# Retention attention and a multiplicative FFN in one kernel: the first dense step as plain products, with the first weights loaded by matrix and the second attention block's first unit moved up

## Chip, core and metric

One core of one Trainium2 chip runs the whole program. The metric is the device time of the program in microseconds (us): the median of several executions. Before the change it is 822.65 us (three runs, 821.73 to 824.22).

## What is computed

The inputs are float32 for the attention and float64 for the weights; the output is float32.

```python
# attention: B=8, H=8, S=576, D=64
scores = matmul(q, k.T) / sqrt(D)
ret    = scores * where(rel >= 0, gamma[h] ** rel, 0)      # causal decay per head
attn   = matmul(ret, v)
x      = attn.transpose(0, 2, 1, 3).reshape(B * S, H * D)  # 4608 x 512
# FFN: w1, w2 512 x 1024; w3 1024 x 1024; w_out 1024 x 512
out    = ((x @ w1) * (x @ w2)) @ w3 @ w_out
```

w3 and w_out are multiplied with each other first (`w3_mm`), so the last two products become one.

## The kernel before, in words

**Attention.** The batch is taken in pairs of two; a unit g is one pair and one chunk of the sequence (a short chunk of 64 rows, then four of 128). The units 0 to 4 are the first pair and are what this change reorders. Each unit goes through the same steps: `load` issues the DMAs of k, q and v (L145), `scale` multiplies q or v by the decay powers (L265 on GpSimd or VectorE, L263 in eight pieces on ScalarE), `front` transposes k and q on TensorE (L279) and copies them out of PSUM on ScalarE (L282), `score` multiplies them (L294) and applies the mask on VectorE (L297), `pv_state` and `pv` make the output (L336, L363) and a function that copies it to `xT` on ScalarE (L370), and `state` adds k and v into the running state (L317, copied at L321).

**Weights.** The float64 weights come in blocks of 128 x 512 numbers: `load_block` issues the DMAs on SyncE's queue into one of five `raw` buffers, and a block is turned into float32 in two halves. `begin_block` makes the exponent (three ScalarE activations L465 to L467, or, for one block, one VectorE instruction L461 and two activations) and the mantissa (VectorE L469, L472); `end_block` joins them (VectorE L483, L496). A generator `conversion` holds that order, and `convert(n)` and `convert_up_to(n)` advance it by so many steps wherever the program calls them. Blocks 0 to 15 are w1 and w2, 16 to 23 w_out, 24 to 39 w3. The first four blocks (key "A") hold 128 columns of w1 and the same 128 of w2 each; the other twelve (key "w12") hold 256 columns of one matrix.

**Dense steps.** `up(i, n, fp)` makes a quarter fp (256 columns of w1 and w2) for one group of 2 x 192 tokens (i, n) by a Strassen-Winograd scheme: seven block products of four matmuls each, 128 x 192, 28 in all (L596), with VectorE additions out of PSUM (L601), two ScalarE copies (L609, L624) and at the end the product of the w1 and the w2 result (L630). It needs the weight sums S1 to S4 of its quarter (`strassen_weights`, four VectorE instructions, L203) and the token sums of its group (`strassen_tokens`, L567). S3 is written over the block A21, and T3 over a block of the tokens. Between its products it advances the conversion (`conv`) and calls what lies in the list `aside`.

**Order.** The order of every engine's instructions is the order in which the program is written (a manual schedule); nothing reorders it later. It matters most in the first 160 us: units 0 to 4, twelve calls of `up` and the conversion of 26 blocks are interleaved by hand, and VectorE and ScalarE run their instructions in that order. Then come the eight `w3_mm` (64 matmuls of 128 x 512, L547), each of which needs one transposed pair of w3 blocks (L500). SyncE's queue carries the loads of k, q, v and of all blocks in program order, and a load whose buffer is still in use holds up those behind it. `keep_busy(n)` multiplies the identity with itself n times (L185), for no result. PSUM gives seven banks to all of this and one to the running state.

Of the kernel before, what the change touches and what calls it, by code (L numbers as in the profile page):

```python
# [8 lines left out]
F32 = mybir.dt.float32  # L9
# [33 lines left out]
def kernel(  # L43
# [338 lines left out]

    blocks = [(("A", r, f), None) for f in range(2) for r in range(2)]
    for fp in range(1, NQ):
        for j, w in enumerate((moe_w1, moe_w2)):
            for r in range(2):
                blocks.append((("w12", fp, j, r), w))
# [5 lines left out]
    def load_block():  # L395
        n = loaded[0]
        if n == len(blocks):
            return
        key, w = blocks[n]
        t = raw.tile([P, CV, 2], I32, tag="raw", name="raw", bufs=5)  # L400
        if key[0] in ("A", "w12"):
            if key[0] == "A":
                _, r, f = key
                t4 = t.rearrange("p (j c n) t -> p j c n t", j=2, c=2)
                parts = [(t4[:, j], w[:, f * P:(f + 1) * P]) for j, w in enumerate((moe_w1, moe_w2))]
            else:
                _, fp, _, r = key
                parts = [(t.rearrange("p (c n) t -> p c n t", c=2), w[:, fp * QC:(fp + 1) * QC])]
            for t2, src in parts:
                src = src[2 * r * P:2 * (r + 1) * P]  # L410
                if r == 0:
                    nc.sync.dma_start(t2, src.rearrange("(c p) n t -> p c n t", p=P))
                else:
                    for half in range(2):
                        nc.sync.dma_start(t2[heads[half]],
                                          src.rearrange("(c a d) n t -> a d c n t", a=2, d=D)[1 - half])
# [12 lines left out]
    def converted_to(n):  # L429
        key, _ = blocks[n]  # L430
        if key[0] == "A":
            return A(0, {(0, 0): "A11", (1, 0): "A12", (0, 1): "A21", (1, 1): "A22"}[key[1:]]).rearrange(
                "p j c n -> p (j c) n")
        if key[0] == "w12":
            _, fp, j, r = key
            return wA[fp // 2][:, r, j, :, fp % 2 * QC:fp % 2 * QC + QC]
        if key[0] == "wo":
            return live["wo"][:, key[1], :]
        _, ft, h = key
        if h == 0:  # L440
            live["w3"] = pools["wst"].tile([P, P // BL, DF // CV, CV // QP], F32, tag="w3", name="w3", bufs=1)
        return live["w3"][:, :, h, :]

    def begin_block():
        n = begun[0]
        t = live["raw", n]
        lo, hi = t[:, :, 0], t[:, :, 1]
        top = t.rearrange("p n t -> p (n t)").bitcast(BF16).rearrange("p (n u) -> p n u", u=4)[:, :, 3]
        e = raw.tile([P, CV], I32, tag="exp", name="e")
        m = raw.tile([P, CV], I32, tag="man", name="m")  # L450
        vec = nc.vector

        half = e.bitcast(BF16).rearrange("p (n u) -> p n u", u=2)[:, :, 1]
        func = mybir.ActivationFunctionType
        if n == 2 * NQ - 1:

            vec.tensor_scalar(out=e, in0=hi, scalar1=1, scalar2=21,  # L461
                              op0=ALU.logical_shift_left, op1=ALU.logical_shift_right)
# [12 lines left out]
        begun[0] += 1  # L475
        yield

    def end_block():
# [8 lines left out]
        while not (key[0] in ("A", "w12") or "wo" in live and (key[0] == "wo" or key[1] < multiplied[0] + 3)):  # L487
            yield "wait"
        out, m, e = converted_to(n), m.bitcast(F32), e.bitcast(F32)
        if key[0] == "A":  # L490
            m, e = (x.rearrange("p (c n) -> p c n", c=4) for x in (m, e))
# [12 lines left out]

        if n >= 4:
            load_block()
        if key[0] == "w12" and key[2:] == (1, 1):
            yield from strassen_weights(key[1])
        yield

    def conversion():

        yield from begin_block()
        while converted[0] < len(blocks):
            if begun[0] < len(blocks) and converted[0] not in (1, 2, 3, 6, 7):
# [15 lines left out]
    def convert(n):  # L533

        for _ in range(n):
            if go_on() is not None:
                return
# [94 lines left out]
            convert(conv)  # L632

    aside, owed, beside = [], [], []

# [175 lines left out]
    keep_busy(4)  # L813
    front(0, "q")
    convert(2)
    score(0)
    scale(0, "v")
    state(0)
    convert_up_to(1)
    pv(0)()  # L820
    load(2, "kqv")
    load_block()
    load_block()
    convert_up_to(2)
    load_block()
    front(1, "k")
    keep_busy(4)
    scale(1, "q", engine=nc.vector)
    front(1, "q")
# [9 lines left out]
    next(weight_sums)  # L839
    pv(1)()  # L840
    keep_busy(4)
    load(3, "v")
    load_block()
    convert_up_to(4)
    token_sums = strassen_tokens(0, 0, nc.vector)
    next(token_sums)
    next(weight_sums)
    list(token_sums)
    list(weight_sums)
    aside.extend([lambda: scale(2, "q", True), lambda: front(2, "k"), lambda: None, lambda: front(2, "q")])  # L850
    scale(2, "v")
    up(0, 0, 0, conv=[0, 0, 2, 2, 2], tail=False, first=True)
    convert(1)
    score(2)
    state(2)
    scale(3, "q", True)
    load(4, "kq")
    front(3, "k")
    convert(3)
    scale(3, "v", engine=nc.vector)  # L860
    copies = pv(2)
    front(3, "q")
    convert(4)
    copies()
# [8 lines left out]
    front(4)  # L873
    convert(1)
    pv(3)()
    list(strassen_tokens(0, 1, nc.vector))
# [517 lines left out]
```

## Time and profile before

| what | value |
|---|---|
| median of three runs | 822.65 us |
| the profiled execution | 821.6 us, span of its instructions 819.5 us |
| TensorE matmul busy | 805.1 us, 98% of the span |
| VectorE busy | 524.4 us, 64% |
| ScalarE busy | 245.3 us, 30% |
| GpSimd busy | 216.2 us, 26% |
| mean granted TensorE clock | 0.994 |
| read from HBM / written | 92.09 MB / 22.28 MB |

The span runs from the first to the last instruction of the profiled execution; the 2.1 us around it belong to start and end. All times below are positions in this span or durations of instructions in it. A busy TensorE need not be at its full clock: the granted clock stands in a column of its own. A wait is listed with what ended it.

### The profile page before, as it was taken

The numbers are of one execution on the slowest core, as the hardware profiler recorded it, in microseconds if no ns is written. First come the engines' busy times: TensorE is split into PE (matmuls) and PEld (weight loads), VectorE is DVE, ScalarE is ACT, GpSimd is POOL, SyncE is SP. The second block draws the span as 40 slices with busy tenths as digits, with TensorE's granted clock in tenths as the row PEclk, the third lists the DMA queues.
The fourth block names the chain that finished last, engine by engine and source line by source line (L and its number), as shares of the span: only waits on it lengthen the run. The fifth ranks groups of instructions, "written<-read, shape, count | busy, mean of one in ns | idle before, by whom it ended". The sixth has DMA issues, their size and how long they took to land.

```text
span 819.5 us, 14497 instructions
## 1 busy us (share of the span) xinstructions
PE 805.1 (98%) x5673; PEld 698.9 (85%) x5673; DVE 524.4 (64%) x789; ACT 245.3 (30%) x442; POOL 216.2 (26%) x147
## 2 busy tenths in 40 slices
PE   7989999999999999999999999999999999999998
PEld 7989999844788999888888888888888888888887
DVE  4899999994446485756545766555575566545633
ACT  4787556572110112113222111233211112232100
POOL 1200020000100503205657013167541213464300
PEclk7999999999999999999999999999999999999999
DMA  9995354468027966755963686458646611342011
GB/s 194 229 222 143 80 119 137 116 201 258 13 55 118 240 173 170 230 139 147 231 175 134 156 139 127 83 156 214 183 162 134 117 52 71 136 168 101 1 52 51
DMA packets 225155, 115.32 MB, mean 141 GB/s; under 512 B 195768, under 2 KB 209336, under 8 KB 225088
## 3 DMA queue, kind: packets, MB, share of 16 engines
q1 hardware_dynamic: 172704, 93.40, 44.2%
q10 hardware_dynamic: 52384, 21.01, 11.8%
q8 instruction: 44, 0.72, 0.4%
q14 instruction: 23, 0.19, 0.1%
HBM read 92.09 MB, written 22.28 MB: 140 GB/s over the span
## 4 chain that ended last, share of the span: by engine, by line
PE 86%; DVE 6%; DMA 3%; SPq 2%; issue 2%; ACT 1%; POOL 0%; ACTq 0%; DVEq 0%; POOLq 0%
PE up L1056 27%; PE po L743 24%; PE up L596 13%; PE ps L547 7%; PE upz L1056 4%; PE xps L363 3%; PE sc L294 3%; DMA ld_v<-in_v_dram 2%; PE st L317 2%; PE xps L336 2%; SPq L893 1%; PE tp L279 1%; DVE pm L297 1%; DVE e L483 1%; DVE m L472 1%
## 5 line engine op out<-in xcount | busy, mean ns | idle before, releaser
L1079 DVE TENSOR_TENSOR room<-up,room 128x512 f32<-128x512 f32 (+1 forms) x168 | 129.1, 784 | 104.4 <-PE up L1056 101.8
L596 PE MATMUL up<-room 128*128 128x192 f32 x864 | 145.2, 328 | 3.3 <-DVE room L601 1.6
L596 PEld LDWEIGHTS up<-room 128*128 128x128 f32 x864 | 140.2, 191 | 6.2 <-DVE room L601 2.2
L743 PE MATMUL po<-w3o,room 128*128 128x256 f32 x544 | 124.4, 383 | 1.8 <-DVE ot L747 1.4
L1056 PE MATMUL up<-room,form 128*128 128x256 f32 x528 | 125.2, 380 | 0.0
L743 PEld LDWEIGHTS po<-w3o,room 128*128 128x128 f32 x544 | 102.2, 190 | 18.0 <-DVE ot L747 2.4
L1056 PE MATMUL up<-room 128*128 128x256 f32 x480 | 114.4, 380 | 0.0
L1056 PEld LDWEIGHTS up<-room,form 128*128 128x128 f32 x528 | 100.6, 191 | 13.3
L1079 POOL TENSOR_TENSOR room<-ring,room 128x512 f32<-128x512 f32 (+1 forms) x60 | 81.7, 1376 | 84.3 <-ACT ring L1078 84.3
L1056 PEld LDWEIGHTS up<-room 128*128 128x128 f32 x480 | 91.5, 191 | 12.1
L265 POOL TENSOR_TENSOR ld_v<-ld_v,gk 128x1024 f32<-128x1024 f32 (+1 forms) x18 | 37.9, 2107 | 220.5 <-DMA ld_v<-in_v_dram 191.3
L747 DVE TENSOR_TENSOR ot<-po,ot 128x256 f32<-128x256 f32 x90 | 37.7, 419 | 50.6 <-PE po L743 50.0
L601 DVE TENSOR_TENSOR room<-up,room 128x384 f32<-128x384 f32 x80 | 44.3, 553 | 39.9 <-PE up L596 39.3
L743 PE MATMUL po<-wB,forms 128*128 128x256 f32 x288 | 67.5, 383 | 0.0
L743 PEld LDWEIGHTS po<-wB,forms 128*128 128x128 f32 x288 | 54.1, 190 | 7.7 <-PE xps L363 0.5
L547 PE MATMUL ps<-wo,w3T 128*128 128x512 f32 x128 | 55.1, 593 | 0.0
L547 PEld LDWEIGHTS ps<-wo,w3T 128*128 128x128 f32 x128 | 24.4, 191 | 30.1 <-issue 29.6
L243 POOL TENSOR_TENSOR bl_q<-bl_q,gqs 128x512 f32<-128x512 f32 (+1 forms) x26 | 26.8, 1053 | 87.2 <-DMA bl_q<-in_q_dram 87.2
L297 DVE TENSOR_TENSOR pm<-sc,mask 128x512 f32<-128x512 f32 (+1 forms) x72 | 42.5, 652 | 4.7 <-PE sc L294 4.7
L1113 POOL TENSOR_TENSOR room<-room 128x1024 f32<-128x1024 f32 x18 | 42.3, 2356 | 1.6 <-DVE room L1079 1.6
L768 DVE TENSOR_TENSOR room<-room,forms 128x512 f32<-128x512 f32 x17 | 13.3, 783 | 43.2 <-PE po L743 43.2
L1078 ACT COPY ring<-up 128x512 f32<-128x512 f32 x24 | 14.0, 585 | 89.4 <-PE up L1056 89.4
(107 smaller groups left out, 958.0 us busy)
## 6 DMA issues: line engine op xcount, KB each, us to landing
form<-kept SPq DMA_DIRECT2D x22, 896.0 KB, 4.6
room<-kept SPq DMA_DIRECT2D x20, 896.0 KB, 4.7
raw<-in_moe_w_dram SPq DMA_DIRECT2D x72, 128.0 KB, 3.0
out_dram<-ot ACTq DMA_DIRECT2D x28, 256.0 KB, 2.2
kept<-form SPq DMA_DIRECT2D x8, 896.0 KB, 5.5
bl_q<-in_q_dram SPq DMA_DIRECT2D x216, 32.0 KB, 2.2
ld_v<-in_v_dram ACTq DMA_DIRECT2D x12, 512.0 KB, 6.8
bl_k<-in_k_dram SPq DMA_DIRECT2D x160, 32.0 KB, 2.8
```

The source lines that it names most:

```text
L243: nc.gpsimd.tensor_tensor(out=part, in0=part, in1=gqs[:, :, n0:n0 + n].unsqueeze(3).to_broadcast([P, NP, n, BL]), op=ALU.mult)
L265: engine.tensor_tensor(out=t, in0=t, in1=gam[:sz, c].unsqueeze(1).unsqueeze(3).to_broadcast([sz, 2, H, D]), op=ALU.mult)
L294: nc.tensor.matmul(sc[j][:sz, p, :sz], kT[hs, b, p, :sz], qT[hs, b, p, :sz], start=True, stop=True)
L297: nc.vector.tensor_mul(pm[:sz, b, j, :, :sz], sc[j][:sz, :, :sz], mask[:sz, :sz].unsqueeze(1).to_broadcast([sz, NP, sz]))
L547: nc.tensor.matmul(ps, live["w3T", ft][:, g, :], live["wo"][:, g, :], start=(g == 0), stop=(g == KF - 1))
L596: nc.tensor.matmul(ps[:, w, :], a[:, w, r, :], b[:, r, :], start=(new and w == r == 0), stop=(w == r == 1), skip_group_check=True)
L601: nc.vector.tensor_add(c[:, to], ps, c[:, sb])
L743: nc.tensor.matmul(ps[nm], a[A][:, f // 2, f % 2, :], live["W"][B][:, f, :], start=(f == 0 and not on), stop=(f == NP - 1), skip_group_che ...
L747: nc.vector.tensor_add(ot[:, to[0], to[1]], ps[nm], ot[:, sb[0], sb[1]])
L1056: nc.tensor.matmul(ps[:, w, :], a[:, w, :], b, start=(pr in (1, 5) and w == 0), stop=True, skip_group_check=True)
L1079: engine.tensor_tensor(out=at(out, l), in0=spread(got), in1=at(old if first and old is not None else out, l), op=ALU.add)
L1113: return lambda: engine.tensor_tensor(out=slab[:, h, p], in0=slab[:, h, p], in1=slab[:, h + 1, p], op=ALU.mult)
```

## The change

The first dense step, `up(0, 0, 0)`, is replaced by two calls of a new function `plain`: all 16 products of the w1 half, copied to SBUF by ScalarE, and later all 16 of the w2 half, multiplied by VectorE with the copies. The first four blocks are loaded like the other w12 blocks: w1 rows 0 to 255, w1 rows 256 to 511, then the same two of w2. Blocks 1, 2 and 3 get the exponent form with one VectorE instruction and two activations. The weight sums of quarter 0 are no longer made as soon as its blocks are there, but before the second dense step. The loads of unit 0's v and unit 1 go ahead of blocks 0 to 3, and all of unit 3's loads ahead of block 5. `front(1, "k")` stands ahead of `pv(0)`; unit 2 and unit 3 are done to the end ahead of the second dense step, which is now `up(0, 1, 0)`, before `up(0, 0, 1)`. The keep-busy matmuls go from 4, 4 and 4 to 8 and 3. Unit 3's v is scaled on GpSimd instead of VectorE.

```diff
-    blocks = [(("A", r, f), None) for f in range(2) for r in range(2)]
-    for fp in range(1, NQ):
+    blocks = []
+    for fp in range(NQ):
         for j, w in enumerate((moe_w1, moe_w2)):
             for r in range(2):
                 blocks.append((("w12", fp, j, r), w))
...
-        if n == 2 * NQ - 1:
+        if n in (1, 2, 3, 2 * NQ - 1):
             vec.tensor_scalar(out=e, in0=hi, scalar1=1, scalar2=21,
                               op0=ALU.logical_shift_left, op1=ALU.logical_shift_right)
...
-        if key[0] == "w12" and key[2:] == (1, 1):
+        if key[0] == "w12" and key[1] and key[2:] == (1, 1):
             yield from strassen_weights(key[1])
...
-            if begun[0] < len(blocks) and converted[0] not in (1, 2, 3, 6, 7):
+            if begun[0] < len(blocks) and converted[0] not in (0, 3, 4, 6, 7):
                 yield from begin_block()
...
+    def plain(i, n, fp, w):
+        m = every.index((i, n))
+        if w == 0:
+            live["ab", i, n] = part_of("ab", 3072 * (m == 1), 2 * KF, TB)
+        ps = [acc.tile([P, 2, TB], F32, tag="acc", name="up") for _ in range(2)]
+        h, half = divmod(fp, 2)
+        x, c = live["xT", m], part_of("sums", 0, 4, 2, TB)
+        for r in range(2):
+            for f in range(2):
+                for b in range(2):
+                    for d in range(2):
+                        at = half * QC + f * P
+                        nc.tensor.matmul(ps[f][:, b, :], wA[h][:, r, w, d, at:at + P], x[:, 2 * r + d, b, :],
+                                         start=(b == r == d == 0), stop=(r == d == 1), skip_group_check=True)
+        for f in range(2):
+            part = c[:, 2 * f:2 * f + 2, 0]
+            if w == 0:
+                nc.scalar.copy(part, ps[f])
+            else:
+                nc.vector.tensor_mul(live["ab", i, n][:, 4 * fp + 2 * f:4 * fp + 2 * f + 2, :], ps[f], part)
...
-    load_block()
     load(0, "v")
-    load_block()
     load(1, "kq")
     load_block()
     load(1, "v")
-    load_block()
+    for _ in range(3):
+        load_block()
     scale(0, "q", engine=nc.vector)
     front(0, "k")
-    keep_busy(4)
+    keep_busy(8)
     front(0, "q")
-    convert(2)
     score(0)
     scale(0, "v")
     state(0)
-    convert_up_to(1)
+    front(1, "k")
     pv(0)()
...
+    keep_busy(3)
+    front(1, "q")
+    convert(2)
+    score(1)
...
+    convert_up_to(3)
+    load_block()
+    plain(0, 0, 0, 0)
+    front(2, "k")
+    convert_up_to(4)
+    load_block()
+    plain(0, 0, 0, 1)
+    scale(2, "q", True)
+    scale(2, "v")
+    front(2, "q")
     convert(2)
-    scale(1, "v")
-    score(1)
-    pv_state(1)
-    convert_up_to(3)
-    convert(2)
-    state(1)
-    load(3, "kq")
-    weight_sums = strassen_weights(0)
...
-    up(0, 0, 0, conv=[0, 0, 2, 2, 2], tail=False, first=True)
...
+    list(strassen_weights(0))
     front(3, "k")
...
+    list(strassen_tokens(0, 0, nc.vector))
     state(3)
+    score(3)
+    pv(3)()
+    list(strassen_tokens(0, 1, nc.vector))
+    convert_up_to(6)
+    aside.extend([lambda: scale(4, "q", True), lambda: None, lambda: front(4, "k"), lambda: front(4, "q")])
+    up(0, 1, 0, conv=2, tail=False)
+    owed.append(2)
     while ("S", 1) not in live:
         convert(1)
-    score(3)
-    aside.append(lambda: scale(4, "q", True))
-    up(0, 0, 1, conv=2, tail=False)
-    owed.append(2)
...
     aside.append(lambda: scale(4, "v", True))
-    up(0, 1, 0, conv=2, tail=False)
+    up(0, 0, 1, conv=2, tail=False)
```

On the engines the change comes to this: TensorE gets four more 128 x 192 matmuls and one keep-busy matmul less; VectorE loses the five additions and the wide product of the first step, gets two products of 128 x 384 and three exponent instructions, and gives one scaling to GpSimd; ScalarE loses three activations; SyncE's queue carries the same bytes with six DMAs less (2 KB instead of 1 KB in one piece).

More of the change, by code (lines that the diff above doesn't have):

```diff
@@ L400, in load_block @@
         t = raw.tile([P, CV, 2], I32, tag="raw", name="raw", bufs=5)
[L401 to L405, printed above, removed]
-            else:
[L407 to L416, printed above, removed]
+        if key[0] == "w12":
+            _, fp, _, r = key
+            t2 = t.rearrange("p (c n) t -> p c n t", c=2)
+            src = w[2 * r * P:2 * (r + 1) * P, fp * QC:(fp + 1) * QC]
+            if r == 0:
+                nc.sync.dma_start(t2, src.rearrange("(c p) n t -> p c n t", p=P))
+            else:
+                for half in range(2):
+                    nc.sync.dma_start(t2[heads[half]],
+                                      src.rearrange("(c a d) n t -> a d c n t", a=2, d=D)[1 - half])
         elif key[0] == "wo":
@@ L430, in converted_to @@
         key, _ = blocks[n]
-        if key[0] == "A":
-            return A(0, {(0, 0): "A11", (1, 0): "A12", (0, 1): "A21", (1, 1): "A22"}[key[1:]]).rearrange(
-                "p j c n -> p (j c) n")
         if key[0] == "w12":
@@ L486, in end_block @@
         key = blocks[n][0]
-        while not (key[0] in ("A", "w12") or "wo" in live and (key[0] == "wo" or key[1] < multiplied[0] + 3)):
+        while not (key[0] == "w12" or "wo" in live and (key[0] == "wo" or key[1] < multiplied[0] + 3)):
             yield "wait"
         out, m, e = converted_to(n), m.bitcast(F32), e.bitcast(F32)
-        if key[0] == "A":
-            m, e = (x.rearrange("p (c n) -> p c n", c=4) for x in (m, e))
         if key[0] == "w12":
@@ L818 @@
     state(0)
-    convert_up_to(1)
+    front(1, "k")
     pv(0)()
+    scale(1, "q", engine=nc.vector)
     load(2, "kqv")
     load_block()
-    load_block()
+    keep_busy(3)
+    front(1, "q")
+    convert(2)
+    score(1)
+    scale(1, "v")
+    pv_state(1)
+    convert_up_to(1)
+    pv(1)()
+    convert(2)
+    state(1)
+    load(3, "kqv")
     convert_up_to(2)
     load_block()
[L826 to L829, printed above, removed]
-    convert(2)
-    scale(1, "v")
@@ L832 @@
-    score(1)
-    pv_state(1)
-    convert_up_to(3)
-    convert(2)
-    state(1)
-    load(3, "kq")
-    weight_sums = strassen_weights(0)
[L839 to L850, printed above, removed]
@@ L851 @@
-    scale(2, "v")
-    up(0, 0, 0, conv=[0, 0, 2, 2, 2], tail=False, first=True)
-    convert(1)
+    convert_up_to(3)
[8 more added lines that the diff above has]
+    front(2, "q")
+    convert(2)
     score(2)
+    convert_up_to(5)
     state(2)
+    load(4, "kq")
     scale(3, "q", True)
-    load(4, "kq")
+    list(strassen_weights(0))
     front(3, "k")
-    convert(3)
@@ L860 @@
-    scale(3, "v", engine=nc.vector)
     copies = pv(2)
+    scale(3, "v")
+    copies()
     front(3, "q")
-    convert(4)
-    copies()
     load(4, "v")
+    list(strassen_tokens(0, 0, nc.vector))
     state(3)
+    score(3)
[5 more added lines that the diff above has]
+    owed.append(2)
     while ("S", 1) not in live:
@@ L868 @@
         convert(1)
-    score(3)
-    aside.append(lambda: scale(4, "q", True))
-    up(0, 0, 1, conv=2, tail=False)
-    owed.append(2)
[L873 to L876, printed above, removed]
     score(4)
     aside.append(lambda: scale(4, "v", True))
-    up(0, 1, 0, conv=2, tail=False)
+    up(0, 0, 1, conv=2, tail=False)
     owed.append(2)
```

## The prediction

> **What bounds the kernel now.** I began with the table of stretches, cut where the granted clock changes and where the dense phases begin. Its columns are the stretch, its length, the busy time of PE, PEld, DVE, ACT and POOL with instruction counts, the granted TensorE clock, the DMA share and GB/s.
>
> ```profile
> core 0: us, PE busy (x) PEld busy (x) DVE busy (x) ACT busy (x) POOL busy (x), PEclk, DMA share, GB/s
> 0.00:11.25 11.25, 7.86 (x81) 7.19 (x81) 3.30 (x10) 3.72 (x7) 1.61 (x8) 1.00 0.92 165
> 11.25:21.48 10.23, 8.75 (x87) 8.37 (x88) 6.84 (x12) 5.54 (x11) 1.23 (x1) 0.50 1.18 227
> 21.48:40.00 18.52, 18.25 (x211) 17.09 (x209) 15.84 (x26) 14.39 (x29) 4.30 (x2) 1.00 1.08 231
> 40.00:80.00 40.00, 37.31 (x438) 34.47 (x440) 37.49 (x65) 32.08 (x68) 0.00 (x0) 1.00 0.83 180
> 80.00:120.00 40.00, 38.84 (x284) 38.21 (x285) 37.60 (x64) 22.04 (x34) 5.99 (x6) 1.00 0.50 107
> 120.00:157.40 37.40, 37.40 (x231) 37.13 (x230) 35.25 (x62) 23.57 (x35) 0.00 (x0) 1.00 0.45 127
> 157.40:212.30 54.90, 54.90 (x129) 24.37 (x129) 34.97 (x52) 26.05 (x37) 3.71 (x4) 1.00 0.65 189
> ```
>
> TensorE is the bound everywhere, but two things are lost early. From 11.25 to 21.48 its clock is halved, so that its 8.75 busy us do some 4.4 us of work. And between 40 and 157 VectorE is 94% busy, so close behind that it could become the pace. Next, the timeline of TensorE (start, duration, instruction, in brackets the idle time before it):
>
> ```profile
> 8.93 0.71 PE L279 MATMUL tp<-ident,ld_q 64*128 64x64 f32 x8 [1.50 <-DVE ld_q L265]
> ...
> 12.53 1.97 PE L317 MATMUL st<-ld_v,ld_k 64*64 64x64 f32 x32 [1.53 <-POOL ld_v L265]
> ...
> 16.14 1.97 PE L279 MATMUL tp<-ident,ld_k 128*128 128x128 f32 x8
> ...
> 28.65 1.47 PE L596 MATMUL up<-room 128*128 128x192 f32 x8
> ...
> 40.11 2.06 PE L294 MATMUL sc<-qT,kT 64*128 64x128 f32 x32
> ...
> 43.18 1.09 PE L279 MATMUL tp<-ident,ld_k 128*128 128x128 f32 x8
> ```
>
> The same eight transposes take 1.97 us at the half clock and 1.09 at the full one; the drop follows two gaps of 1.5 us. The list of TensorE's waits gives the other losses inside the part that is rewritten:
>
> ```profile
> PE up L596 <- DVE room L601: 1.6, 2, 1.2
> PE up L596 <- DVE room L203: 1.4, 1, 1.4
> PE st L317 <- DVE ld_v L265: 0.7, 1, 0.7
> ```
>
> Last, where the rewritten part joins the rest: the transposed w3 pairs on VectorE, and the first matmul that uses one.
>
> ```profile
> 145.03 1.24 DVE L500 STREAM_TRANSPOSE w3T<-w 128x1024 f32<-128x1024 f32 x1
> 154.24 1.24 DVE L500 STREAM_TRANSPOSE w3T<-w 128x1024 f32<-128x1024 f32 x1
> 162.75 1.25 DVE L500 STREAM_TRANSPOSE w3T<-w 128x1024 f32<-128x1024 f32 x1
> ```
>
> The w3 matmuls start at 157.4 and use a pair each 54.9/8 = 6.87 us: pair 2 is due at 171.1 and there at 164.0. VectorE has 7 us to spare there, and gains 0.6 us a pair (6.24 us from pair to pair). After 212 TensorE waits for no transfer, so what is gained before the w3 phase is kept.
>
> **The change, part by part.** I follow TensorE's new order with the durations of these rows.
>
> *Start, to the first dense product (28.65 before).* Unit 0's v now lies second on SyncE's queue; before, block 0 (0.52 MB) went ahead and v landed at 10.5. At the 154 GB/s of the first 10 us that is 3.4 us earlier; scaled on GpSimd (1.90) it is there at 9.0, ahead of the end of score 0 at 11.0. So the wait of 1.53 goes. The gap before q's transposes (1.50) gets four more keep-busy matmuls (1.16 for four, till 8.6; the scaled q comes at 8.9, nothing is delayed). If the clock then stays up, from 11.0 on: state 1.0, k transposes 0.95, pv 1.0, three keep-busy 0.8, q transposes and the copy behind them 1.2, score 2.0, the two steps of pv 1.05 and 1.9, state 1.0, so the first dense product at 21.9. That is 6.75 us earlier: 1.53 of the wait, 1.0 of a keep-busy group that is gone, the other 4.2 the half clock.
>
> How the clock would react no row shows directly. Bounds: it may drop as before (0 of 4.2), or not at all. I take not at all, as gaps are left of only some 0.25 us, and between 40 and 50 units with the same steps and gaps up to 0.7 us ran at 1.00. Against it: the steps of unit 0 are smaller (64x64), and the stretch 14.7 to 18.1, without a gap and full of pv and transposes, did not bring the clock back. [...]
>
> *Plain products.* 32 matmuls for 28: 4 x 0.327 = +1.3. The second half of the w1 products needs block 1. Its bytes and those ahead of it are units 0 and 1 (0.79 + 1.57) and two blocks (1.05), 3.41 MB. Before moved 1.54, 3.94, 6.02 and 8.46 MB in 10, 20, 30 and 40 us (154, 240, 208, 244 GB/s), so it lands at about 18. But ScalarE makes its exponent only after the copies of pv(1) (20.9 + 1.1), 1.45 us, and VectorE then joins, 1.38: ready at 24.9, where the first eight products end at 24.5. +0.4. Blocks 2 and 3 are joined at 28 and 29.5, the w2 half starts at 28.5 after the transposes of k2: no wait. Score 2 starts at 21.9 + 5.25 + 0.4 + 0.95 + 5.25 + 1.25 = 35.0, before 40.1: **-5.1**.
>
> *Units 2 and 3 and the next two steps.* The stalls 0.73, 1.41 and 0.47 us go: v3 is scaled by GpSimd (1.9 to 2.4) and lands, with 8.13 MB ahead and itself, at 38.7, so it is ready at 41 for a state at 43.5. What is late next is VectorE. It idles from 29.5 to 33.7, as its two products of the w2 half stand ahead of block 4 in its queue, and again before the token sums, which wait for the copies of pv(3) (49.5). From there its order is: token sums 2.2, blocks 5, 6 and 7 at 2.4 each (0.42 + 0.69 + 0.68 + 0.69, starts overlapping by some 0.05 each), S sums 2.7, five additions at 0.47 and a product, mask 4 (2.45), the same again with blocks 8 to 10, and the end of `up(0, 0, 1)` at 78. The seventh product of each step needs the bank of the third addition: that comes at 59.6 and 72.9, TensorE waits 0.9 and 1.6 there, and 0.5 for the token sums. So 2.6 go and 3.0 come; `up(0, 1, 1)` starts at about 77.9 for 82.8: **-4.9**.
>
> *To the w3 phase.* VectorE has 5 x 0.554 + 0.953 - 2 x 0.554 = 2.6 less in the first step, 3 x 0.42 = 1.3 more for exponents, and 1.2 less for v3. Two blocks and a transpose (2 x 2.5 + 1.24 = 6.2) are now written behind the last addition before the w3 phase, where they were ahead of it. Without that VectorE would be late by what it lost in its idle time; with it, it keeps abreast. TensorE's order there is unchanged; I leave its stall of 1.16 us at 119 as it is. Pair 1 is then ready 2.1 + 5.5 = 7.6 us after the start of the phase, due after 6.87: **+0.7**. From pair 2 on VectorE gains. SyncE's queue has the 16 small loads (9.56 us) ahead of block 18 instead of 20; these blocks had 5 us or more of lead. Without that lead, up to 9.6 us would show; I take 0.
>
> Sum: -4.9 + 0.7 = -4.2, from 821.6 to 817.4 for one execution like the profiled one. The median of the runs is 1.05 above that execution; I go half way, to **817.8**.
>
> **Rivals.** *The clock drops all the same.* For it: unit 0's small steps and transposes. Against: no gap is left. The 4.2 go, but later work then waits less for VectorE, some 0.8 back: 817.8 + 3.4 = 821.2, no change.
>
> *VectorE's idle time is not made up.* GpSimd slows it: two sums of L203 took 2.99 us beside the scaling at 32.3, for 2.0 elsewhere, and v3's scaling now falls on the S and token sums. With that and another stall of the kind of 119.4 (1.16): 820.0, slightly faster or the same.
>
> *The transfers of unit 3 come too late, and it is slower.* Its v is needed scaled at 43.5, and everything behind it hangs on it, as the second dense step needs pv(3)'s tokens. VectorE then idles too, so a delay is paid in full. By the bytes it lands at 38.7. If the queue moved only 154 GB/s, as in the first 10 us, it would land at 2.5 + 8130/154 = 55.3 and be ready at 57.5: 14.0 us late, 9.8 slower than before. It turns slower when v lands later than 41.3 + 4.2 = 45.5 us, below 8130/43.0 = 189 GB/s. For it: v2 landed at 32.3 with 6.03 MB, 202 GB/s from 2.5 on. Against: that queue was then held up by buffers, with dips to 86 GB/s, and now every buffer of these loads is free long before. Time at 170 GB/s: v at 50.3, 4.8 behind the turning point, 822.65 + 4.8 = 827.4.
>
> **How the numbers follow.** Forecast 0.55, clock 0.17, VectorE 0.10, transfers 0.18. A measurement of this kernel cannot tell less than about 0.3%, 2.5 us, from no change, so same is 820.2 to 825.1. Faster: the forecast and half of VectorE's case, 0.60; same: the clock, the other half, 0.22; slower: the transfers, 0.18. The forecast's own range is 814 to 820. Below, if all of VectorE's new waits are hidden too (3.0 + 0.7), 814.1; above, the clock's case with another 1.2 us stall, 822.4. The range is 813.5 to 822.5; the transfers' case is left out.
>
> **What would show it.** Right: a granted clock of 1.00 from 10 to 22 us; the first dense product near 22 and score 2 near 35; no wait for v0; TensorE waiting for L590, VectorE's additions, between 55 and 75; the w3 matmuls starting near 152 to 153, with one short wait at their second group. Wrong: 0.50 in that stretch; TensorE waiting for v3 (L317) or k3, or the first dense product later than 25; a w3 start later than 157.

## The result, and the profile after

The changed kernel takes **819.56 us** (median of 10 runs, 818.04 to 821.41), the kernel before 822.37 us in the same comparison (10 runs, 820.7 to 824.22). The ratio is 0.9968, with an interval of 0.9955 to 0.9981: faster by 2.8 us, where the forecast of 817.8 lies 4.6 below. The profiled execution of the changed kernel took 820.0 us (span 818.3) against 821.6, so 1.6 us less where 4.2 were worked out. The medians differ by more than these two executions because the profiled one lies 0.4 us above its median after the change and 0.8 us below it before.

First the table of stretches of the changed kernel, cut at the same places as before (columns as above), up to the start of the w3 phase, which is now 155.54.

```profile
0.00:11.25 11.25, 9.08 (x99) 8.41 (x101) 2.83 (x10) 2.58 (x5) 2.84 (x8) 1.00 1.03 143
11.25:21.48 10.23, 7.83 (x147) 6.87 (x142) 6.59 (x9) 5.51 (x10) 1.81 (x1) 1.00 1.02 235
21.48:40.00 18.52, 18.05 (x161) 17.44 (x163) 11.65 (x21) 11.53 (x24) 1.99 (x2) 0.91 1.08 203
40.00:80.00 40.00, 38.09 (x454) 34.42 (x452) 37.61 (x65) 29.63 (x64) 2.37 (x1) 1.00 0.78 171
```

From 11.25 to 21.48 the clock is 1.00 instead of 0.50, as forecast, and 147 matmuls are done there instead of 87. But the 7.83 busy us leave 2.4 idle, and in the next stretch the mean clock is 0.91. The timeline of TensorE in the changed kernel shows why:

```profile
8.37 0.71 PE L279 MATMUL tp<-ident,ld_q 64*128 64x64 f32 x8
...
10.92 1.15 PE L317 MATMUL st<-ld_v,ld_k 64*64 64x64 f32 x32 [0.48 <-POOL ld_v L265]
...
18.22 1.10 PE L336 MATMUL xps<-qT,sb 64*64 64x128 f32 x32
21.62 3.53 PE L363 MATMUL xps<-pm,ld_v 128*64 128x128 f32 x32 [2.30 <-POOL ld_v L265]
...
26.02 5.79 PE L638 MATMUL up<-room 128*128 128x192 f32 x32
...
39.00 2.06 PE L294 MATMUL sc<-qT,kT 64*128 64x128 f32 x32 [0.24 <-ACT qT L282]
```

The gaps of unit 0 are closed and the steps follow each other up to 19.3. There TensorE waits 2.30 us for unit 1's v, which `pv(1)` (L363) needs scaled. In slices of 0.25 us the granted clock is 0.50 from 21.46 to 24.88, so `pv(1)` takes 3.53 us instead of 1.97. The first dense product starts at 26.02 (28.65 before, 21.9 forecast), score 2 at 39.00 (40.11 before, 35.0 forecast).

The chain of waits of the changed kernel (start, duration, what; the pieces of under 0.1 us between them are left out) says what v of unit 1 waited for:

```profile
3.42 4.61 SPq L145
8.07 2.77 SPq L406
10.88 8.72 DMA ld_v<-in_v_dram
19.67 1.91 POOL ld_v L265
21.62 3.53 PE xps L363 x32
```

SyncE spends 4.61 us on the issue of unit 1's q and 2.77 on that of block 0, so v is issued only at 10.88; 8.72 us later it has landed, and GpSimd scales it in 1.91.

For the rest of the changed part, the list of TensorE's waits of the changed kernel (sum, times, longest):

```profile
PE up L585 <- DVE room L590: 1.8, 2, 1.5
PE ps L536 <- DVE w3T L489: 0.6, 1, 0.6
```

and the transposed w3 pairs on VectorE's timeline:

```profile
154.25 1.23 DVE L489 STREAM_TRANSPOSE w3T<-w 128x1024 f32<-128x1024 f32 x1
161.86 1.25 DVE L489 STREAM_TRANSPOSE w3T<-w 128x1024 f32<-128x1024 f32 x1
168.01 1.25 DVE L489 STREAM_TRANSPOSE w3T<-w 128x1024 f32<-128x1024 f32 x1
```

The stalls for L203 and for v3 (L317) are gone. The additions (now L590) hold TensorE twice, 1.53 us at 77.33 and 0.26 at 126.71. The stall of 1.16 at 119, in the fourth call of `up` counted from `up(0, 1, 1)`, is gone too; the 0.26 stands in the fifth. `up(0, 1, 1)` starts at 81.77 (82.83 before, 77.9 forecast) and the w3 phase at 155.54 (157.38 before), where pair 1 is late once, by 0.57 us.

### The profile page after: what moved, and what is told of

It reads as the page before. It is cut to its first block, busy times and chain, and to the rows that moved or that the text cites. A ratio compares the mean times of both kernels' runs of the same rounds, so it can differ in the third digit from the quotient of the medians.

```text
span 818.3 us, 14501 instructions
## 1 busy us (share of the span) xinstructions
PE 805.2 (98%) x5679; PEld 696.7 (85%) x5679; DVE 526.5 (64%) x787; ACT 243.3 (30%) x439; POOL 219.6 (27%) x148
## 4 chain that ended last, share of the span: by engine, by line
PE 80%; DVE 9%; DMA 4%; SPq 3%; issue 2%; ACT 1%; POOL 0%; ACTq 0%; DVEq 0%
PE up L1059 27%; PE po L754 23%; PE up L585 9%; PE ps L536 6%; PE upz L1059 4%; PE xps L363 3%; PE sc L294 3%; DMA ld_v<-in_v_dram 2%; PE st L317 1%; PE up L638 1%; DMA bl_q<-in_q_dram 1%; PE xps L336 1%; DVE room L203 1%; DVE room L590 1%; SPq L896 1%
## 5 line engine op out<-in xcount | busy, mean ns | idle before, releaser
L585 PE MATMUL up<-room 128*128 128x192 f32 x808 | 135.5, 328 | 2.0 <-DVE room L590 1.8
L585 PEld LDWEIGHTS up<-room 128*128 128x128 f32 x808 | 131.1, 190 | 5.0 <-DVE room L590 2.6
L754 PE MATMUL po<-w3o,room 128*128 128x256 f32 x544 | 124.1, 382 | 1.5 <-DVE ot L758 1.5
L754 PEld LDWEIGHTS po<-w3o,room 128*128 128x128 f32 x544 | 102.0, 190 | 17.7 <-DVE ot L758 2.6
L1059 PEld LDWEIGHTS up<-room 128*128 128x128 f32 x480 | 91.2, 190 | 12.4
L265 POOL TENSOR_TENSOR ld_v<-ld_v,gk 128x1024 f32<-128x1024 f32 (+1 forms) x19 | 39.6, 2086 | 227.9 <-DMA ld_v<-in_v_dram 91.7
L758 DVE TENSOR_TENSOR ot<-po,ot 128x256 f32<-128x256 f32 x90 | 37.7, 419 | 49.5 <-PE po L754 48.5
L754 PE MATMUL po<-wB,forms 128*128 128x256 f32 x288 | 67.5, 382 | 0.0
L590 DVE TENSOR_TENSOR room<-up,room 128x384 f32<-128x384 f32 x75 | 41.4, 552 | 33.1 <-PE up L585 32.3
L754 PEld LDWEIGHTS po<-wB,forms 128*128 128x128 f32 x288 | 54.0, 190 | 7.9 <-PE xps L363 0.5
L774 ACT COPY ot<-po 128x256 f32<-128x256 f32 x18 | 6.7, 372 | 107.7 <-PE po L754 73.9
```

The costliest lines, as they stand in the source:

```text
L265: engine.tensor_tensor(out=t, in0=t, in1=gam[:sz, c].unsqueeze(1).unsqueeze(3).to_broadcast([sz, 2, H, D]), op=ALU.mult)
L585: nc.tensor.matmul(ps[:, w, :], a[:, w, r, :], b[:, r, :], start=(new and w == r == 0), stop=(w == r == 1), skip_group_check=True)
L590: nc.vector.tensor_add(c[:, to], ps, c[:, sb])
L754: nc.tensor.matmul(ps[nm], a[A][:, f // 2, f % 2, :], live["W"][B][:, f, :], start=(f == 0 and not on), stop=(f == NP - 1), skip_group_che ...
L758: nc.vector.tensor_add(ot[:, to[0], to[1]], ps[nm], ot[:, sb[0], sb[1]])
L1059: nc.tensor.matmul(ps[:, w, :], a[:, w, :], b, start=(pr in (1, 5) and w == 0), stop=True, skip_group_check=True)
```

## The experiments

**How the executions are compared.** Two things are read from each profiled execution: the start of the w3 phase, and the sum of TensorE's listed waits after 240 us (L754 for L758, L763 or L774, and a few smaller; added up from parts rounded to 0.1), a part that the change doesn't touch. In e6, where all lies some 10 us later, a wait of 0.37 at 246.1 is left out, as it stands ahead of 240 in the others. Time less both is 662.2 us before and 662.7 to 664.0 in all others, so these two say where an execution's time went, to within some 1.3 us.

| kernel | median, us (runs) | ratio to before, interval | first dense product | w3 start | waits after 240 | profiled, us |
|---|---|---|---|---|---|---|
| before | 822.37 (10) | 1 | 28.65 | 157.38 | 2.0 | 821.6 |
| after | 819.56 (10) | 0.9968 [0.9955, 0.9981] | 26.02 | 155.54 | 1.7 | 820.0 |
| e1 v1 first | 819.1 (6) | 0.9962 [0.9949, 0.9974] | 23.58 | 154.28 | 2.4 | 820.14 |
| e2 gap filled | 819.89 (12) | 0.9971 [0.9961, 0.9981] | 24.47 | 154.98 | 3.7 | 822.27 |
| e3 v1, v3 first | 823.58 (12) | 1.0021 [1.0008, 1.0033] | 23.10 | 156.02 | 0.5 | 819.32 |
| e4 start alone | 822.3 (12) | 0.9997 [0.9986, 1.0007] | 28.70 | 158.98 | 1.3 | 823.0 |
| e5 keep-busy 4 | 822.36 (12) | 0.9997 [0.9984, 1.001] | 26.75 | 156.09 | 2.5 | 822.05 |
| e6 Strassen kept | 831.28 (4) | 1.0118 [1.0101, 1.0134] | 31.59 | 166.82 | 2.6 | 832.11 |
| e7 v3 on VectorE | 819.68 (12) | 0.9975 [0.9962, 0.9988] | 23.96 | 153.99 | 1.4 | 818.23 |
| e8 no keep-busy | 821.14 (12) | 0.9994 [0.9983, 1.0006] | 25.54 | 155.67 | 1.6 | 820.21 |
| e9 (e3 again) | one run | | 23.49 | 156.92 | 2.1 | 822.86 |
| e10 (e5 again) | one run | | 25.73 | 155.39 | 3.9 | 822.76 |
| e11 copy on VectorE | 821.62 (11) | 0.9994 [0.9985, 1.0004] | 25.97 | 155.57 | 1.2 | 820.5 |
| e12 e1 and copy | 820.8 (12) | 0.9984 [0.9975, 0.9992] | 24.42 | 155.13 | 4.1 | 823.21 |

The theory was that unit 1's v and the clock drop behind it took the missing 4 us; the rival, that other transfers would have taken them anyway.

**e1: unit 1's v ahead of block 0**

```diff
     load(1, "kq")
-    load_block()
     load(1, "v")
-    for _ in range(3):
+    for _ in range(4):
         load_block()
...
-    convert(2)
     score(1)
+    convert(2)
```

> The changed kernel with unit 1's v loaded ahead of block 0 (instead of behind it), and the first two conversion steps behind score(1), so that VectorE's queue does not stop at a block that now lands later. Theory 'arrival': in the changed kernel TensorE waits 2.30 us for v of unit 1 (landed 19.67) and the clock halves in the next 3.4 us, 1.7 us more; with v 0.52 MB earlier (about 2.4 us at 215 GB/s, near 17.3) the wait is gone, the clock stays 1.00 and the first dense product is near 22.5 instead of 26.0. But v of unit 3 was ready at 47.1 and used at 47.15, and its bytes do not move, so state(3) will wait some 2.5 to 3.5 us there and most of the gain is given back: 818 to 819.5, against 819.56. Rival 'carried through': nothing bounds it later, 815.5 to 816.5. Rival 'VectorE': nothing changes, 819.6, and the new wait is for VectorE's additions (L590), not for L317.

The median is 0.5 us under that of the changed kernel in the table, well inside the intervals. TensorE's timeline in this kernel:

```profile
19.34 1.97 PE L363 MATMUL xps<-pm,ld_v 128*64 128x128 f32 x32 [0.16 <-POOL ld_v L265]
...
23.58 2.84 PE L638 MATMUL up<-room 128*128 128x192 f32 x16 [1.34 <-DVE room L485]
27.70 2.84 PE L638 MATMUL up<-room 128*128 128x192 f32 x16 [1.29 <-DVE room L485]
```

The wait for v1 is 0.16 us, and the clock stays at 1.00. But 1.34 + 1.29 = 2.6 us of waits for blocks 0 and 1 (L485 joins a block) come in its place. Block 0, now behind v1, landed at 19.66 instead of some 16.3. Block 1 is not late by its transfer: VectorE and ScalarE take it up right behind block 0, and VectorE begins block 2 ahead of joining it. Of the 4.1 us between forecast and measurement at the first dense product 2.4 are won, at `up(0, 1, 1)` still 1.3 (80.50). So the gain was lost at the blocks, and not at v3, as the theory had it: v3 was scaled 0.06 us ahead of its use and not waited for.

**e2: the gap filled.** The loads stay, and eight more identity products keep TensorE busy while it waits.

```diff
     convert_up_to(1)
+    keep_busy(8)
     pv(1)()
```

> The changed kernel with eight keep-busy matmuls ahead of pv(1), into the 2.30 us that TensorE waits for unit 1's v. They do no work. Theory 'the gap drops the clock': granted clock 1.00 throughout in every run, the half-clock stretch (3.4 us from 21.5) gone, the first dense product near 24.5 instead of 26.0, and the time like that of the runs of the changed kernel with a mean clock of 1.000 (818.0 to 819.1), so about 818.6, against 819.56 over all its runs. Rival 'harmless': the work behind is bound by transfers or VectorE, so the clock there costs nothing: 819.6. Rival 'the clock falls for the small steps, not for the gap': 0.50 in that stretch as before, 820.

In TensorE's timeline of this kernel:

```profile
19.35 2.05 PE L185 MATMUL idle<-ident 128*128 128x128 f32 x16
21.64 1.97 PE L363 MATMUL xps<-pm,ld_v 128*64 128x128 f32 x32 [0.23 <-POOL ld_v L265]
...
47.27 1.15 PE L317 MATMUL st<-ld_v,ld_k 128*64 128x64 f32 x32 [1.36 <-POOL ld_v L265]
```

v1 comes as late as in the changed kernel, but the clock does not fall, and `pv(1)` takes 1.97 us: here the gap caused the drop. Its mean clock is 0.999 or 1.000 in all 12 runs; in half of the changed kernel's 10 it is 0.998, which is what one stretch of 3.41 us at half clock makes (3.41/2 of 818). Those five took 820.5 us on average, the other five 818.7. That the drop alone makes this difference is not shown: e7 has a trace of an execution with a mean clock of 1.000, and there more is different. Yet the median is not lower here. The 1.2 us gained at score 2 (37.80) are given back at v3, for which TensorE now waits 1.36, and the w3 phase starts only 0.56 earlier.

**e3: unit 3's loads ahead of block 4 as well**

```diff
     (the edits of e1, and)
-    load_block()
     keep_busy(3)
...
     load(3, "kqv")
+    load_block()
     convert_up_to(2)
...
-    convert(2)
     score(2)
+    convert(2)
```

> As e1_v1_first, and unit 3's loads also ahead of block 4, whose first conversion steps go behind score(2). In e1 TensorE no longer waits for any v, but 1.34 and 1.29 us for blocks 0 and 1, and state(3) at 45.9 had no wait. Theory 'the sum of the bytes ahead sets the start': nothing to gain from v3, block 4 lands some 7 us later (1.57 MB) and is due near 40, so VectorE starts the weight sums later: 819.1 to 820.5. Rival 'v3 was the next limit': 818 or less.

Nothing is gained: the median lies above both ranges of the expectation and is the worst of those with plain products. Score 2 starts at 37.26, but TensorE waits 1.6 us for q3's eight pieces on ScalarE and 0.55 for its copies, and the w3 phase starts at 156.02, later than in e1. The profiled execution was the fastest of its runs (819.32), so the median was left without a cause; e9 takes that up.

**e4: the start alone.** Before, with v0 first on the queue and eight identity products in the first gap.

```diff
-    load_block()
     load(0, "v")
     load_block()
+    load_block()
     load(1, "kq")
...
     front(0, "k")
-    keep_busy(4)
+    keep_busy(8)
```

> The kernel before with the start alone: unit 0's v ahead of block 0 (two blocks behind it) and eight instead of four keep-busy matmuls in the first gap; the Strassen first step and everything later as before. Theory 'arrival and clock': the wait of 1.53 us for v0 shrinks to some 0.5, the clock does not halve at 11.25, and most of the 4.2 us half-clock loss and the wait are gained at the first dense product (28.65 before), as far as blocks 2 and 3 (landing near 25) and the sums on VectorE allow: 26 to 27 there, 820 to 821 in all, so that about half of the whole change's gain of 2.8 us is this start. Rival 'blocks': the first step waits for VectorE's blocks and sums anyway, 822.4, no gain. Rival 'all of it': 819 or less, and the plain products and moved units bring nothing.

No gain. TensorE's timeline:

```profile
15.11 1.83 PE L279 MATMUL tp<-ident,ld_k 128*128 128x128 f32 x8 [1.40 <-DMA ld_k<-in_k_dram]
...
19.81 1.06 PE L279 MATMUL tp<-ident,ld_q 128*128 128x128 f32 x8 [1.16 <-DVE ld_q L265]
...
28.70 5.37 PE L596 MATMUL up<-room 128*128 128x192 f32 x32
```

With two blocks ahead of unit 1's loads, the waits move from v0 and q0 to k1 and q1; the clock is at 0.50 for 3.4 us instead of 10.2, and the first dense product starts where it did. The time is that of the rival 'blocks', but not its reason: no wait for a block or a sum stands at the first dense product. Behind it the waits for v3 and for the weight sums are 1.21 and 1.90 us (0.73 and 1.41 before), and the w3 phase starts 1.6 us later.

**e5: four identity products instead of eight**

```diff
-    keep_busy(8)
+    keep_busy(4)
```

> The changed kernel with four instead of eight keep-busy matmuls in front of unit 0's q transposes, so that a gap of 1.0 us stands there again, followed by the gaps of 0.21 and 0.48. [...] But TensorE then waits less for v of unit 1 (landed 19.67), so part is hidden: first dense product 26 to 27.5, 820 to 821.5. Rival 'filling was not needed': clock 1.00 there, first dense product at 26.0, 819.6.

The expected 26 to 27.5 count on half speed behind the first gap, an estimate of the author's that neither trace of this kernel shows. q0 came early enough that the gap was only 0.28 us (0.18 in e10), and the clock did not fall there (1.00 up to 22.75): in this trace and in that of e10 the four extra products are not what keeps it up. v1 was ready 0.66 us later than after (0.46 of that as its scaling took 2.36 us for 1.90) and the first dense product came 0.7 later. The w3 phase starts 0.55 later than after, yet the median lost the whole gain. e10 asks where.

**e6: Strassen in the place of the plain products.** The weight and token sums and the step of 28 matmuls stand where the second plain half stood; both halves are taken out.

```diff
-    plain(0, 0, 0, 0)
     front(2, "k")
...
-    plain(0, 0, 0, 1)
+    list(strassen_weights(0))
+    list(strassen_tokens(0, 0, nc.vector))
+    up(0, 0, 0, tail=False)
```

> The changed kernel with the first dense step as the Strassen scheme again, in the place of the second plain call: block order, loads, keep-busy and the order of the units stay changed, 28 products instead of 32, and the weight sums and token sums of the first step stand ahead of it again. Theory 'w1 first is what lets TensorE start': the sums need all four blocks (the fourth is joined at 33.0 in the changed kernel) and then 2.7 us, so the step starts some 8 to 9 us later than the plain one (26.0), with only k transposes of unit 2 in between, and the clock drops in the gap: 825 to 829. Rival 'the loads and the units' order make the gain, the products do not matter': 818.3, 1.3 us less than 819.56 for the four matmuls saved.

11.7 us slower than after by the medians. In TensorE's timeline:

```profile
29.86 1.94 PE L279 MATMUL tp<-ident,ld_k 128*128 128x128 f32 x8 [3.95 <-DMA ld_k<-in_k_dram]
...
38.25 10.18 PE L585 MATMUL up<-room 128*128 128x192 f32 x48 [3.89 <-DVE room L556]
```

TensorE has nothing to do until k2 and then until the token sums; the granted clock is at 0.50 from 22.1 to 25.5 and again from 29.0 to 42.6. The w3 phase starts 11.3 us later than after. In this order of loads the plain products are what makes the start work.

**e7: v3 scaled on VectorE, as before**

```diff
-    scale(3, "v")
+    scale(3, "v", engine=nc.vector)
```

> The changed kernel with unit 3's v scaled on VectorE again (1.22 us) instead of GpSimd. In the changed kernel GpSimd's 2.37 us stand beside VectorE's weight sums of quarter 0, which take 4.32 us there where the same four take 2.01 + 0.69 later. Theory 'what GpSimd takes off VectorE it gives back by slowing it': the sums take 2.7, VectorE is busy 1.2 longer by the scaling, about 0.4 less in all: 819.2 to 819.8, no difference, state(3) waiting up to 0.7 for VectorE. Rival 'relief': 820.8 and VectorE's additions later by 1.2.

No difference from after that the intervals show, as the theory had it. The four sums took 2.74 us, the scaling 1.22, and TensorE waited 0.73 for it:

```profile
42.33 2.74 DVE L203 TENSOR_TENSOR room<-room 128x512 f32<-128x512 f32 x4
44.99 1.22 DVE L265 TENSOR_TENSOR ld_v<-ld_v,gk 128x1024 f32<-128x1024 f32 x1
```

The profiled execution has the earliest w3 start of all (153.99), for reasons that are not the edit: TensorE's first 16 keep-busy products ran slower (3.50 us for 2.05), so that it came to `pv(1)` 1.9 us later, and v1's scaling began at 17.83 for 19.67, with the same loads in the same order. So there was no gap there, no drop, and a mean clock of 1.000. Here, as with the changed kernel, the runs with a clock of 1.000 are the fast ones: four at 818.5 us on average, against eight with 0.997 or 0.998 at 820.4. The fast half of the changed kernel's runs may have started like this one; no trace of it was kept.

**e8: no keep-busy at all**

```diff
-    keep_busy(8)
...
-    keep_busy(3)
```

> The changed kernel without either group of keep-busy matmuls (11 fewer, 3.0 us of TensorE time). The loads are the same, so v of unit 1 still lands near 19.7 and the first dense product cannot come before its use. Theory 'the clock is what the keep-busy matmuls buy': gaps of some 2.1 and 0.8 us return, the clock halves from about 11 for 3.4 to 10 us, and is still or again at one half behind the wait for v: first dense product 26.5 to 28, 821 to 824, like the kernel with four instead of eight (822.4 against before 821.8 in the same comparison). Rival 'they only take time': 819 or less, clock at 1.00.

By the ratios (0.9994 and 0.9968) some 2.1 us above after: the gain is nearly gone, as the theory had it, but not by its way. In the timeline TensorE runs at about half speed up to some 20.5, as eight transposes take 1.97 us for 1.09, `pv(0)` 1.97 for 1.15 and score 1, at 18.83, 2.92 for 2.06 (the 20.5 is worked out from the last):

```profile
13.14 1.97 PE L279 MATMUL tp<-ident,ld_k 128*128 128x128 f32 x8
15.03 1.97 PE L363 MATMUL xps<-pm,ld_v 64*64 64x64 f32 x32
```

Nevertheless the first dense product starts at 25.54, a little before that of after: TensorE at half speed merely fills the time that it would wait for v1. That is the second sign that the transfers, and not the clock, set the start. This execution took 820.21 us, as long as that of after; what its slower runs lose stands in no trace.

**e9 and e10: e3 and e5 once more**, unchanged, for a second trace each.

> The kernel of the run with unit 1's v and unit 3's loads ahead (median 823.58, profiled execution 819.32, its fastest) once more, for a second trace. If its other executions are slower because the waits of the start vary with the transfers, this one lies at 821.5 to 824.5 and shows up(0, 1, 1) later than 82.23, at 83.5 to 86, with longer waits for block 0 or 1 or for q3 or v3. If they are slower because of later work, up(0, 1, 1) stays at 82 to 83 and the waits after 240 us, 0.24 us in the first trace, add up to 2 us or more. At 819 to 820 it tells nothing.

> The kernel of the run with four keep-busy matmuls in the first gap (median 822.36, profiled execution 822.05) once more. If the clock at the start is what varies, the first dense product moves from 26.75 to 28 or later, with transposes or products at twice their duration between 8 and 22 us, and the time is 822.5 to 824.4; if later waits decide, the start repeats (26 to 27) and the waits after 240 us, 2.2 us in the first trace, tell the difference to the first trace's 822.05 to within 0.5 us.

Both came out near their medians. e9 is 3.5 us slower than e3: 0.9 by the start of the w3 phase, as the clock falls behind the waits for q3 (0.50 from 47.6 to 51.0, state 3 in 1.98 us for 1.15 and score 3 in 2.66 for 2.06; in e3 it did not, although these waits were longer, 1.64 us for 1.30), 1.6 by waits after 240 us, and 1.0 by neither. e10 starts the w3 phase even earlier than after, and still takes 2.8 us more, 2.2 of them in those waits. So the later part decides in e10 and makes about half of the difference in e9. The largest of them in e10, first on ScalarE's timeline:

```profile
262.94 4.98 ACTq L812 DMA_DIRECT2D out_dram<-ot  x3
267.96 0.37 ACT L1175 COPY room<-xps 128x256 f32<-128x256 f32 x1 [9.10 <-DMA out_dram<-ot]
...
269.29 0.37 ACT L774 COPY ot<-po 128x256 f32<-128x256 f32 x1
```

and then on TensorE's:

```profile
269.71 1.99 PE L754 MATMUL po<-w3o,room 128*128 128x256 f32 x8 [1.87 <-ACT ot L774]
```

The issue of three output transfers holds ScalarE for 4.98 us; behind it stand four copies and the copy that TensorE waits for. In after the same issue came 0.87 us earlier and took 3.98 us, and the copy was in time:

```profile
262.07 3.98 ACTq L812 DMA_DIRECT2D out_dram<-ot  x3
```

**e11 and e12: that copy (L774, all 18 of them) on VectorE**, in the changed kernel and in e1.

```diff
-        nc.scalar.copy(ot[:, 0, 0], ps[1])
+        nc.vector.tensor_copy(ot[:, 0, 0], ps[1])
```

> The changed kernel with the first copy of each output product group (L774, 18 of them) on VectorE instead of ScalarE. Theory: part of what the start gains is lost again after 240 us, as this copy stands on ScalarE behind the issue of three output transfers, which hold ScalarE 4.0 us from 262.1 in the trace of the changed kernel and 5.0 us in the second trace of the kernel with four keep-busy matmuls, where TensorE then waits 1.9 us. Then the waits for L774 go, the executions lie closer together, and the median falls by 0.3 to 1.0 us to 818.5 to 819.3. Rival: VectorE is the late one there (L758, 1.5 us of waits in the changed kernel), so that the copy makes those waits longer and the median stays at 819.6 or rises to 821.

> The same copy on VectorE in the kernel with unit 1's v ahead of block 0 (median 819.1). Theory: that kernel reaches the w3 phase 1.3 us earlier than the changed one (154.3 for 155.5) but had a median only 0.5 us lower, with waits of 1.7 us for L758 and 0.5 us for L774 after 240 us; without the latter 818.0 to 818.9. Rival, with waits at L758 that grow instead: 819.1 or more. If both kernels come out alike, the first 155 us no longer decide the time.

The theory falls: the waits on ScalarE go, but both medians rise, by 2.1 and 1.7 us. For the rival's cause there is one trace on either side. In e12, whose profiled execution is its slowest, the waits for VectorE's additions (L758) are 3.4 us, where e1 had 1.7; in e11's profiled execution, one of its faster ones, they are 0.5 (1.5 after), and 0.9 stand for the copy itself on VectorE. e12 stays 0.8 us below e11, as e1 stayed 0.5 below after.

No kernel tried is faster than the changed one by more than the intervals allow.

## Why the prediction was nearly right

The sign held, and the range, which reached from 813.5 into no change. Of the mechanism, the closed gaps of unit 0 and the early dense work held; the start was sized too large, and the prediction's own sign of being wrong, a first dense product later than 25, came true (26.02). Two sums do not add up as written, by 0.2 and 0.1 us: -5.1 with 2.6 gone and 3.0 come is -4.7, and half way from 817.4 to the median is 817.9. And the half clock before did not follow two gaps of 1.5 us: it began at 11.23, 0.2 us into the second.

- *Start, "so the first dense product at 21.9", 6.75 us earlier.* Measured 26.02, 2.63 earlier: this is the step that failed. v0 did come earlier (the wait went from 1.53 to 0.48, which was for GpSimd, whose scaling waited for the decay powers until 8.97). "As gaps are left of only some 0.25 us" was wrong: the sum set the arrival of v0, block 1 and v3 against their use, but never that of v1 against `pv(1)`. Its own method would not have warned: v1 with all ahead of it is 2.88 MB, which had moved at about 16.7 us by the rates of the trace after (143 GB/s to 11.25, 235 then), yet v1 had landed only at 19.6. SyncE issued q1, block 0 and v1 one after the other (at 3.42, 8.07 and 10.88, q1 in 4.61 us), and all three were under way at once, as q1 was taken up at 13.61 and block 0 at 16.31; so the byte count gave an earliest time here and not the landing. The 4.1 us are 2.30 of wait, 1.6 for `pv(1)` at half clock, and 0.2 in smaller pieces.
- *The clock.* The forecast "not at all" held up to 19.3 us: no half clock where the gaps were filled (e2 shows it again at the next gap). The rival "the clock drops all the same" was wrong on the cause; that its size, 3.4 us, is near the 4.1 that v1 cost at the first dense product is chance.
- *"Ready at 24.9" for block 1.* The executions in which TensorE comes earlier show that limit: the second eight products start at 27.70 in e1, 27.77 in e2 and between 27.2 and 29.0 in the five others with such a wait (e3, e7, e8, e9, e12). Had v1 been in time, some 2.8 us of the forecast's start would still have been lost here (27.70 against 24.9). In e1 block 1's exponent began on ScalarE at 23.80, behind the joining of block 0, and VectorE began block 2 ahead of joining it; the sum had neither. e1 measured it: 1.26 us more at the w3 phase, and 0.5 in the median, inside the intervals, is all that unit 1's v is worth alone.
- *Plain products.* The 5.25 us for a half were right (5.37 in the timeline, whose ends overlap); e6 prices them against Strassen in the same place at 11.7 us.
- *Units 2 and 3.* The waits for L203 and v3 went. v3 landed at 44.7, not 38.7, and was ready at 47.09 for a state at 47.15: in time only because TensorE itself was 4 us late. In e2, with TensorE 1.2 us earlier at score 2 and v3 0.5 later, the wait is there. The rival of late transfers was right on what binds, with a turning point (45.5) 0.8 us away. Of the 3.0 us of new waits 1.53 and 0.24 came, and 0.7 inside `pv(3)`, which took 2.65 us for 1.97 while its weight loads waited for VectorE's mask. The 0.9 in the first step did not come, and no run shows why; that TensorE was late is not the reason, as e1 and e7, where it is earlier, have none there either, and the same 1.54 in the second.
- *To the w3 phase.* -1.84 instead of -4.9. Of that, 1.11 are there at score 2 and 1.06 at `up(0, 1, 1)`: the moved units lose as much as they gain. The other 0.78 come behind it, where the stall of 1.16 at 119, counted as staying, went and 0.26 came. The prediction has no term for that: it is luck, and no run shows its cause. Pair 1: 0.57 measured for +0.7.
- *"What is gained before the w3 phase is kept."* In the sum of one execution, yes: -1.84 + 0.57 - 0.3 of later waits = -1.6. But the later waits differ by up to 3.6 us between executions (0.5 to 4.1 in the table), and they are 2.2 of the 2.8 us by which e10 lies above after, and 1.6 of the 3.5 by which e9 lies above e3. Why a given order of the start leads to more of them was not found; that the first 155 us and the transfers of the output part are connected at all is only argued.

So the likeliest account is: the change closed the gaps of unit 0 and gave TensorE dense work before all four blocks were there; it ran into the transfers of unit 1 and block 0 and VectorE's work on blocks 0 and 1, and no order of the loads tried (e1, e3) moves that limit by more than about 1 us of the total. The start alone gains nothing (e4), and without the plain products the new order loses 11.7 us (e6); how the 2.8 us divide among the other parts of the change was not tested.

## What to carry to other kernels

When the gaps at the start were closed, the next transfer in the queue (v1, 2.30 us of wait) became the limit here: list every load with its issue, landing, scaling and first use, the small ones too, before the gain is summed, and put what a step gains no higher than the next such date. A transfer's landing is read from issue and landing of its neighbours, not from bytes over a rate (16.7 by bytes for v1, 19.6 measured), and it varied: with the same loads ahead, v1's scaling began between 19.4 and 19.9 in seven executions and at 17.83 in e7. Where waits of 0.5 to 4 us vary in a later part, gains under 2 us are judged by a milestone ahead of that part in the traces and by a dozen runs, not by one profiled execution.

## What the hardware did that was not expected

- **The half clock came in pieces of 3.41 us.** Read in slices of 0.25 us it lasted 3.4 us after, in e4, e5, e9, e10 and e11 (after in slices of 0.05: 21.46 to 24.87), 10.2 before (three times 3.41) and 13.7 at the end of e6 (four times). Why it fell after one gap and not after another was not shown: the 3.41 us ahead of 21.46 hold 1.26 us of products and 2.1 of idle time, those ahead of e9's drop only 1.3 of idle time between transposes, while single gaps of 1.34 and 1.36 us in e1 and e2 among other products did no harm, nor did gaps of 1.6 us together in e3, between the same transposes as in e9.
- **The clock column was blind at the start.** In e8 it reads 1.00 throughout its profiled execution, while eight transposes took 1.97 us for 1.09; the duration of a known group told more. Up to about 11 us the same holds for e7 (16 identity products in 3.50 us for 2.05) and e12 (from 8 to 11 three or four matmuls in each slice of 0.25 us, as in e7, where after has four or five from 6.75 to 8.00). Over e8's 12 runs the mean clock is 0.992 to 0.994 in eight and 0.999 or 1.000 in four, at the same times (821.4 and 821.2 us on average).
- **VectorE was slower beside GpSimd's scaling.** One instruction at 19.83 (L474, two operands of 128 x 512) took 2.29 us beside a scaling at 19.67, and 0.68 to 0.69 without; four sums of L203 took 4.32 us beside one at 44.72, and 2.74 in e7, where none runs beside them.
